# Two V transfers of group 1 made as 120 and 8 partitions each, in a chunk-attention and squared-ReLU FFN kernel on one Trainium2 core

## The chip, the core and the metric

The kernel runs on one core of a Trainium2 chip. TensorE (PE, with weight loads listed as PEld), VectorE (DVE), ScalarE (ACT) and GpSimd (POOL) run their own instruction queues; SyncE (SP) mostly issues DMA transfers, which the core's 16 DMA engines carry out. The metric is the device time of one execution in microseconds; lower is better. A time is the median of several runs. The profile and the trace come from one execution of their own.

## What is computed

The inputs are `q`, `k`, `v` of 8 batches x 8 heads x 576 positions x 64 elements in float32, and the weights `w_in` (512 x 2048) and `w_out` (2048 x 512). Attention stays within chunks of 64 positions; the FFN runs over all 4608 tokens. Cut to what matters:

```python
scores = scale * np.matmul(q_c, k_c.transpose(0, 1, 2, 4, 3))
scores = scores - np.max(scores, axis=-1, keepdims=True)
attn = np.exp(scores)
attn = attn / (np.sum(attn, axis=-1, keepdims=True) + 1e-09)
out = np.matmul(attn, v_c)
...
x = attn_out.transpose(0, 2, 1, 3).reshape(B * S, H * D)
h = np.maximum(x @ w_in, 0.0)
return (h * h @ w_out).astype(np.float32)
```

## The kernel before

**Groups and blocks.** The 4608 tokens are cut into 18 groups of 256 tokens (four chunks each), and two groups make a block of 512 tokens. For each group the kernel transposes q and k, makes the scores (`scores`, line 464), multiplies the exponentials with V (`values`, line 496), normalizes (`out_of_x`, line 438) and transposes the result x, so that the FFN can use it. The FFN of block j runs while the attention of the next blocks is made in between. From block 4 on, the FFN products are made with fewer multiplications (lines 601 to 892); the change doesn't touch that.

**Order.** The program is written with a manual schedule: the instructions of each engine run in the order in which the code emits them. The framework adds the waits between engines.

**The opening.** Lines 967 to 991 are block 0's attention, ahead of any FFN work, written out by hand. `go(pieces([0, 1]))` (line 967) issues all transfers of groups 0 and 1 on SP's queue: first q and k of both groups (line 266, four transfers of 512 KB), then V of group 0, then V of group 1, as `v_pieces` gives them. `load_w_in(0, n_cast=2)` follows, the first eighth of w_in (line 329, 512 KB, into a float32 staging tile `w_st`); GpSimd casts its first half to bf16 (line 334), ScalarE its second half (line 333). TensorE's order is then: transposes of q and k, scores of group 0 and 1, the values of group 0 in two halves, those of group 1 in two halves (`AV(1, [0])`, `AV(1, [1])`, line 510), with transposes of x in between (`transpose_x_early`, line 521), and small filler matmuls on the identity (`keep_busy`, line 433). After the last transposes come the matmuls of the first FFN (line 579), which need w_in in bf16.

**V's tiles.** The 64 rows of a chunk and four heads of 64 elements make a tile's content for one parity of the heads. The even heads of a group lie in `v_even[g % 5]`, whose two halves `[:, 0]` and `[:, 1]` hold 128 positions each; the odd heads lie in `v_odd` tiles, moved by one chunk against the even ones. A transfer of 128 partitions is 128 KB: in each partition four pieces of 256 B, one per head. For group 1 there are four transfers, in this order on SP's queue: `even[0]` (line 308, 128 partitions), `odd[0]` (line 312, 128 partitions), `even[1]` (line 308, 128 partitions), `odd[1]` (line 312, 64 partitions, 64 KB). The second half of the values, `AV(1, [1])`, reads `even[1]` and both odd tiles; the first half reads `even[0]`, `odd[0]` and a tile of group 0.

**After the opening.** Lines 993 to 1002 issue the rest of w_in, w_out and the loads of the next groups on the same queue, each w_in or w_out piece into one of five staging tiles as they come free.

Of the kernel before, what the change touches and what calls it, by code (L numbers as in the profile page):

```python
# [144 lines left out]
def kernel(  # L145
# [9 lines left out]
    nc = tc.nc  # L155

    B, H, S, D = q.shape
# [17 lines left out]
    chunks = whole[:-2] + rest + whole[-2:]  # L175
# [64 lines left out]
    v_even = [w_pool.tile([128, 2, n_hp, D + 1], FP32, name=f"ve_sb{i}") for i in range(NV)]  # L240
    v_odd = [w_pool.tile([128, n_hp, D + 1], FP32, name=f"vo_sb{i}") for i in range(NO)]
# [5 lines left out]
    def runs(g):  # L247

        for t in range(2):
            (b, s), (b1, s1) = chunks[g][2 * t:2 * t + 2]  # L250
            if b == b1:
                yield t, 0, 2 * CH, b, s
            else:
                yield t, 0, CH, b, s
                yield t, CH, CH, b1, s1
# [28 lines left out]
    odd_tile, odd_loads = {}, {}  # L284
    n_odd = 0
    for g in range(n_grp):
        if is_whole(g):
# [3 lines left out]
            b, s = chunks[g][0]  # L291
# [12 lines left out]
    def v_pieces(g):  # L304

        even, odd = [], []
        for t, p, m, b, s in runs(g):
            even.append(lambda t=t, p=p, m=m, b=b, s=s: nc.sync.dma_start(  # L308
                out=v_even[g % NV][p:p + m, t, :, 0:D],
                in_=v[b, 0::2, s:s + m, :].rearrange("h s d -> s h d")))  # L310
        for n, p, m, b, s in odd_loads[g]:
            odd.append(lambda n=n, p=p, m=m, b=b, s=s: nc.sync.dma_start(  # L312
                out=v_odd[n % NO][p:p + m, :, 0:D],
                in_=v[b, 1::2, s:s + m, :].rearrange("h s d -> s h d")))
        if g < 2:
            yield from [even[0], *odd[:-1], even[1], odd[-1]]
        else:
            yield from even + odd

# [607 lines left out]
    def pieces(grps):  # L927
        for g in grps:
            yield from qk_pieces(g)
        for g in grps:  # L930
            yield from v_pieces(g)
# [72 lines left out]
    for j in range(QUADS):  # L1004
# [33 lines left out]
        else:  # L1038
# [4 lines left out]
            if j == 2:  # L1043
                loads, go_slots = itertools.chain(*map(v_pieces, nxt), pieces(far)), [
                    *range(16), *range(27, 36)]
                slots = {SC: (6, 10), AV: (12, 22), XT: (15, 28), CQ: (20, 22), CK: (21, 24), TD: (24, 26)}
                for f in (CQ, CK, TD):
                    for i, g in enumerate(far):
                        at(slots[f][i], f, g)
                phases.append(out_j)  # L1050
            else:
                loads, go_slots = pieces(far), range(11)
                at(11, C, far[0])
                at(13, CQ, far[1])
                at(13, TD, far[0])
                slots = {SC: (2, 4), AV: (7, 10), XT: (13, 15)}
# [40 lines left out]
    for j in range(QUADS, n_blk):  # L1097
# [7 lines left out]
        if j == QUADS:  # L1105
            g = blocks[QUADS + 1][1]
# [116 lines left out]
```

## Time and profile before

| what | value |
|---|---|
| time, median of 3 runs | 279.12 us (278.87 to 279.75) |
| the profiled execution, its own time | 278.37 us |
| its span in the trace | 276.6 us |
| PE busy | 265.3 us, 96% of the span |
| DVE, ACT, POOL busy | 199.3, 170.1, 90.7 us |
| DMA | 55.07 MB moved, mean 199 GB/s |
| DMA, mean rate in the first two fortieths of the span | 216 and 260 GB/s |
| granted TensorE clock | 1.0 in every stretch |

How to read it: times are from the start of the span. A line number names the line of the kernel that issued the instruction; `SPq` is SP's issue of a transfer, `DMA` the time in which a transfer is under way. A group's line has what it writes, an arrow, what it reads, and the number of instructions; the bracket behind it gives how long the engine stood idle before it, and what ended that. A wait is put down to the one event that came last.

### The profile page before, as it was taken

The page shows a single profiled execution, that of the slowest core. Times are in us where ns is not written, and L with a number is a line of the kernel's source. Part 1 is how long each engine was busy: PE and PEld are TensorE (multiplying, and loading weights), DVE is VectorE, ACT ScalarE, POOL GpSimd, SP SyncE. Part 2 cuts the span into 40 slices and gives each one's busy share as a digit, 9 for nine tenths or more (in the row PEclk, how much of TensorE's full clock was granted, in tenths as well). Part 3 has the DMA queues.
Part 4 walks back from the last instruction along what each step waited for, and adds up shares of the span by engine and source line. Part 5 has one row for each costly group of instructions (what it writes and reads, how often), then busy time and mean ns, then how long its engine had stood idle before and what let it go on. Part 6 is the DMA issues. An engine that isn't in the chain of part 4 may idle for free.

```text
span 276.6 us, 7949 instructions
## 1 busy us (share of the span) xinstructions
PE 265.3 (96%) x3274; PEld 203.9 (74%) x3277; DVE 199.3 (72%) x365; ACT 170.1 (61%) x302; POOL 90.7 (33%) x122
## 2 busy tenths in 40 slices
PE   2889999999999999999999999999999999999994
PEld 2764445888774588447888888888898888888884
DVE  1457415999538692599989998799679877994852
ACT  1657514894458883867678765566856664756430
POOL 2048734350270012140245224551434312431600
PEclk9999999999999999999999999999999999999999
DMA  7999999999999999998999999697995330220223
GB/s 216 260 373 383 366 318 262 325 209 162 278 209 206 245 246 231 285 240 121 229 228 199 217 236 198 116 214 198 254 195 162 78 76 2 89 62 9 71 83 114
DMA packets 133943, 55.07 MB, mean 199 GB/s; under 512 B 102160, under 2 KB 129808, under 8 KB 133904
## 3 DMA queue, kind: packets, MB, share of 16 engines
q1 hardware_dynamic: 131136, 46.02, 70.9%
q0 software_dynamic: 2624, 8.39, 9.7%
q8 instruction: 26, 0.43, 0.6%
q10 hardware_dynamic: 144, 0.13, 0.1%
q14 instruction: 13, 0.11, 0.1%
HBM read 36.70 MB, written 9.44 MB: 167 GB/s over the span
## 4 chain that ended last, share of the span: by engine, by line
PE 82%; DVE 8%; DMA 4%; SPq 4%; issue 1%; ACT 0%; POOL 0%
PE ps_ffn L657 23%; PE ps_out L780 22%; PE ps_ffn L579 13%; PE ps_ffn L780 12%; PE ps_ffn L901 5%; DVE gT L598 4%; PE ps_att L510 2%; DMA w_st<-in_moe_w_in_dram 2%; PE ps_att L483 2%; PE ps_att L540 2%; DMA qkT<-qkb 2%; SPq L266 1%; SPq L308 1%; SPq L312 1%; DVE x L443 1%
## 5 line engine op out<-in xcount | busy, mean ns | idle before, releaser
L579 PE MATMUL ps_ffn<-xT,w_in_bf 128*128 128x512 bf16 (+1 forms) x328 | 58.0, 333 | 0.1
L780 PEld LDWEIGHTS <-w_st 128*128 128x128 bf16 x512 | 48.8, 98 | 6.6 <-DVE w_st L614 0.5
L665 DVE CUSTOM_DVE_ANT_0 relu<-ps_ffn,w_st 128x512 f32<-128x512 f32 x60 | 39.3, 685 | 12.8 <-PE ps_ffn L657 11.4
L598 DVE TENSOR_TENSOR gT<-relu 128x256 bf16<-128x256 bf16 (+2 forms) x68 | 34.6, 543 | 18.0 <-ACT relu L590 17.5
L579 PEld LDWEIGHTS <-w_in_bf 128*128 128x128 bf16 x328 | 31.1, 98 | 21.4 <-POOL w_in_bf L334 0.2
L590 ACT ACTIVATE relu<-ps_ffn 128x256 bf16<-128x256 f32 (+2 forms) x82 | 39.5, 502 | 10.3 <-PE ps_ffn L579 9.6
L657 PE MATMUL ps_ffn<-qk_st,w_in_bf 128*128 128x256 bf16 x240 | 35.3, 273 | 0.0
L657 PEld LDWEIGHTS <-w_in_bf 128*128 128x128 bf16 x320 | 30.6, 98 | 4.0 <-issue 0.3
L809 POOL DMA_DIRECT2D out_dram<-o_sb x24 | 17.6, 733 | 44.7 <-DVE o_sb L614 24.6
L780 PEld LDWEIGHTS <-gT 128*128 128x128 bf16 x296 | 28.6, 98 | 3.3
L780 PE MATMUL ps_out<-w_out_bf,w_st 128*128 128x256 bf16 x240 | 30.8, 273 | 0.0
L699 ACT ACTIVATE w_st<-ps_ffn 128x512 f32<-128x512 f32 x20 | 11.9, 598 | 27.5 <-PE ps_ffn L657 27.5
L443 DVE TENSOR_TENSOR x<-ps_att,recs 128x512 bf16<-128x512 f32 x36 | 24.9, 692 | 1.2
L657 PEld LDWEIGHTS <-qk_st 128*128 128x128 bf16 x240 | 22.6, 98 | 2.9
L676 POOL TENSOR_TENSOR qk_st<-relu 128x512 bf16<-128x512 f32 x10 | 10.3, 1034 | 41.6 <-DVE relu L665 38.1
L657 PE MATMUL ps_ffn<-xT,qk_st 128*128 128x256 bf16 x160 | 23.9, 273 | 0.0
L494 ACT ACTIVATE e<-ps_att 128x1024 bf16<-128x1024 f32 x18 | 18.4, 1023 | 8.6 <-PE ps_att L483 8.6
L676 POOL TENSOR_TENSOR gT<-relu 128x512 bf16<-128x512 f32 x10 | 10.3, 1033 | 36.9 <-DVE relu L665 36.9
L449 POOL CAST qkb<-qk_st 128x1024 bf16<-128x1024 f32 x12 | 14.8, 1236 | 13.3 <-DMA qk_st<-in_q_dram 13.3
L674 ACT ACTIVATE gT<-relu 128x512 bf16<-128x512 f32 x28 | 17.7, 631 | 0.0
L780 PE MATMUL ps_ffn<-w_out_bf,w_st 128*128 128x256 bf16 x144 | 17.7, 273 | 0.0
L614 DVE TENSOR_TENSOR w_st<-gT,w_st 128x1024 bf16<-128x1024 bf16 x26 | 17.5, 708 | 0.0
(92 smaller groups left out, 430.5 us busy)
## 6 DMA issues: line engine op xcount, KB each, us to landing
qk_st<-in_q_dram SPq DMA_DIRECT2D x16, 512.0 KB, 5.8
out_dram<-o_sb POOLq DMA_DIRECT2D x28, 256.0 KB, 3.9
qk_st<-in_k_dram SPq DMA_DIRECT2D x24, 256.0 KB, 5.3
ve_sb<-in_v_dram SPq DMA_DIRECT2D x32, 128.0 KB, 3.9
w_st<-in_moe_w_in_dram SPq DMA_DIRECT2D x8, 512.0 KB, 6.0
w_st<-in_moe_w_out_dram SPq DMA_DIRECT2D x8, 512.0 KB, 5.4
vo_sb<-in_v_dram SPq DMA_DIRECT2D x24, 128.0 KB, 3.3
qk_st<-in_k_dram SPq DMA_DIRECT2D x4, 512.0 KB, 5.9
```

The costliest lines, as they stand in the source:

```text
L443: nc.vector.tensor_tensor(out=x, in0=o[:, :, :, 0:D], in1=rec.to_broadcast([128, 2, n, D]), op=ALU.mult)
L494: nc.scalar.activation(out=e_out, in_=s_in, func=AF.Exp, scale=scale)
L579: nc.tensor.matmul(out=h[:, 0:n], lhsT=w_in_bf[:, dt, ft * 128:(ft + 1) * 128], rhs=xT[:, c // 128:(c + n) // 128, dt, :], start=(dt == 0) ...
L590: nc.scalar.activation(out=rl[:, 0:n], in_=h[:, 0:n], func=AF.Relu)
L598: nc.vector.tensor_tensor(out=dst, in0=src, in1=src, op=ALU.mult)
L614: nc.vector.tensor_tensor(out=out, in0=in0, in1=in1, op=op)
L657: nc.tensor.matmul(out=bank[:, f * GT:(f + 1) * GT], lhsT=a[:, dt, ft * 128:(ft + 1) * 128], rhs=b[:, :, dt, :], start=(first and f == 0 a ...
L665: nc.vector._custom_dve(TENSOR_ADD_SAT, out=out, in0=in0, in1=in1, s0=BIG, s1=0.0)
L674: engine.activation(out=dst, in_=r, func=AF.Square)
L676: engine.tensor_tensor(out=dst, in0=r, in1=r, op=ALU.mult)
L780: nc.tensor.matmul(out=out_ps, lhsT=lhsT, rhs=b[:, i, :], start=(first and i == 0 and (last or t == 0)), stop=(i == HF - 1), skip_group_ch ...
L809: dma.dma_start(out=out[t0:t0 + GT, col:col + HD].rearrange("(t p) d -> p t d", p=128), in_=o_sb.rearrange("p (t d) -> p t d", d=HD))
```

## The change

For group 0 the order stays. For group 1 the first even and the first odd transfer, 128 partitions each, are replaced by two transfers each: 8 partitions (120 to 127) and then 120 partitions (0 to 119). The two that follow, `even[1]` and `odd[-1]`, stay as they were and behind them. The other groups stay as they were.

```diff
-        if g < 2:
+        if g == 0:
             yield from [even[0], *odd[:-1], even[1], odd[-1]]
+        elif g == 1:
+            for tile_, heads, s in ((v_even[1][:, 0], 0, chunks[1][0][1]),
+                                    (v_odd[odd_loads[1][0][0]], 1, odd_loads[1][0][4])):
+                for p, m in ((120, 8), (0, 120)):
+                    yield lambda t=tile_, h=heads, s=s, p=p, m=m: nc.sync.dma_start(
+                        out=t[p:p + m, :, 0:D],
+                        in_=v[chunks[1][0][0], h::2, s + p:s + p + m, :].rearrange("h s d -> s h d"))
+            yield from (even[1], odd[-1])
         else:
             yield from even + odd
```

## The prediction

> **What bounds the kernel now.** I began with the page: the span, the shares by engine, and the DMA queues.
>
> ```profile
> span 276.6 us, 7949 instructions
> PE 265.3 (96%) x3274; PEld 203.9 (74%) x3277; DVE 199.3 (72%) x365; ACT 170.1 (61%) x302; POOL 90.7 (33%) x122
> ...
> q8 instruction: 26, 0.43, 0.6%
> ```
>
> Then busy time by stretches, cut where the first FFN matmul starts (17.42 us) and just before the end; the second column is the length, the third PE.
>
> ```profile
> 0.00:17.42 17.42, 10.63 (x244) 8.38 (x245) 6.20 (x13) 7.51 (x11) 2.13 (x24) 1.00 1.03 264
> 17.42:270.00 252.58, 251.58 (x3004) 193.04 (x3008) 191.73 (x350) 162.19 (x291) 88.53 (x98) 1.00 0.81 197
> ```
>
> From 17.42 us to 270 us TensorE is idle for 252.58 - 251.58 = 1.0 us in all. So what the opening gains or loses passes to the end almost unchanged, and whatever the change does later to SP's queue must first eat the slack of loads that already arrive in time. The question is when the first FFN matmul starts. The chain of waits, in order of time, gives one answer:
>
> ```profile
> 8.76 0.63 SPq L308
> 9.39 0.04 issue
> 9.44 0.55 SPq L312
> 9.98 0.04 issue
> 10.03 0.58 SPq L308
> 10.61 0.04 issue
> 10.65 0.60 SPq L312
> 11.26 0.04 issue
> 11.30 5.40 DMA w_st<-in_moe_w_in_dram
> 16.70 0.06 issue
> 16.75 0.62 POOL w_in_bf L334
> 17.38 0.05 issue
> 17.42 14.01 PE ps_ffn L579 x72
> ```
>
> SP issues group 1's four V transfers (8.76 to 11.26), then the first piece of w_in; it lands at 16.70, POOL casts it, PE starts. The chain shows one predecessor only. The timeline of the opening shows a second, equally late:
>
> ```profile
> 14.46 0.22 PE L510 MATMUL ps_att<-ve_sb,e 64*64 64x65 bf16 x2
> ...
> 15.11 0.69 DVE L443 TENSOR_TENSOR x<-ps_att,recs 128x512 bf16<-128x512 f32 x1
> ...
> 15.23 0.22 PE L510 MATMUL ps_att<-ve_sb,e 64*64 64x65 bf16 x2 [0.45 <-DMA ve_sb<-in_v_dram]
> ...
> 15.62 0.21 PE L510 MATMUL ps_att<-vo_sb,e 64*64 64x65 bf16 x1 [0.17 <-DMA vo_sb<-in_v_dram]
> ...
> 15.97 0.21 DVE L442 RECIPROCAL recs<-ps_att 128x8 f32<-128x8 f32 x1 [0.18 <-PE ps_att L510]
> ...
> 16.22 0.69 DVE L443 TENSOR_TENSOR x<-ps_att,recs 128x512 bf16<-128x512 f32 x1
> ...
> 16.96 0.40 PE L521 MATMUL ps_ffn<-ident,x 128*128 128x128 bf16 x4
> ...
> 17.42 2.51 PEld L579 LDWEIGHTS <-w_in_bf 128*128 128x128 bf16 x21 [0.23 <-POOL w_in_bf L334]
> ```
>
> The second half of group 1's values waits for V until 15.62, DVE normalizes until 16.22 + 0.69 = 16.91, and the last transposes end at 16.96 + 0.40 = 17.36, 0.06 us before the FFN. Two chains tie, so a gain needs both.
>
> Why is the data so late? The views merge packets, so I took this from the trace's packet records (us from the span's start):
>
> ```
> queue 8 (instruction): one packet, 16384 B, starts 12.50, takes 1.288
> 256 B packets of V: 4096 in all; 4048 of them are over by 13.41
> the other 48 start from 13.77 on and are over at 14.85, one after another
> w_in piece 0, end of each engine's part: 14.70 to 15.21 for fifteen engines, 16.30 for one
> first packet of the first q transfer: 1.87; w_in piece 0's first packet: 12.96
> ```
>
> One DMA engine stands still while it fetches instructions, with exactly 32 + 16 = 48 V packets before it: its shares of SP's last two V transfers (128 partitions x 4 heads / 16 = 32 packets, and the half-size one). It ends V 14.85 - 13.41 = 1.44 us after the others, and the first w_in piece 16.30 - 15.21 = 1.09 us after them. The queue 8 row says the same in the mean: 0.6% of 16 engines x 276.6 us, over 26 packets, is 1.0 us each, on one engine.
>
> The Trainium skill ("Runtime: NRT & Kernel Launch", section "Instruction fetch mechanics") says that each engine's program is refilled in blocks of 16 KiB, 256 instructions. The trace agrees: (3274 + 3277) / 256 = 25.6, and there are 26 packets, so these would be TensorE's, and their time is set by TensorE's progress.
>
> **The change, part by part.** It leaves the bytes alone. Four issues stand where two stood, and the two transfers that it splits are the ones *ahead* of the 48 late packets. The late ones (line 308's second, line 312's half-size one) stay as they are, on all 16 engines.
>
> *SP's issues.* No transfer of 8 or 120 partitions is in the trace. The nearest are the crowded V issues above (0.55 to 0.63, plus 0.04) and an uncrowded one:
>
> ```profile
> 33.30 0.46 SPq L308 DMA_DIRECT2D ve_sb<-in_v_dram  x1
> ```
>
> Low end: four at 0.50 from 8.76, then two at 0.50: the last two V issues start at 10.76 and 11.26, w_in at 11.76, 0.46 later than now. High end: 0.67 each, so 11.44, 12.11 and 12.78, 1.48 later. I take 0.55 each (10.96, 11.51, 12.06): the two 8-partition transfers give the queue a sixteenth of the packets, so the crowd should ease. The first transfer's first packet came 1.87 - 0.75 = 1.12 us after its issue began. So w_in's packets could start at 12.06 + 1.12 = 13.18, or 13.90 at the high end; the late engine takes them up only at 14.85. *Cost: nothing*, covered by that engine's lateness. Without this cover the other engines' end would move from 15.21 by 13.18 - 12.96 = 0.2 up to 0.9 us, still not past 16.30.
>
> *Packets.* If the freed engine is the one that fetches, it loses 64 packets, and runs out of work before 12.50. What it gains depends on how many of its last 48 pass before the fetch. The second-last V transfer, issued at 10.96, can show packets from 12.08; 0.42 us at (0.60 us per V transfer / 32 =) 19 ns each is 22 packets. With the issue ends: 32 packets (11.88) or none (12.56). The remaining ones took (14.85 - 13.77) / 48 = 22 ns each, so V would end 0.5 us earlier (0 to 0.7), and w_in behind it.
>
> *What that is worth.* DVE still works on the first half until 15.11 + 0.69 = 15.80. The second reciprocal can move from 15.97 to 15.80 at best: 0.17 us, then the products, the transposes (end 17.19) and the FFN. w_in needs only 0.17 of the 0.5 us. So -0.17 if packets pass before the fetch, 0 if none do. Both are about as likely by the row above: -0.08.
>
> *Waits.* Values of group 1 now wait for two transfers more. On PE's queue nothing shows such an extra wait alone; the nearest row is that of the waits ahead of w_in's issues (min, median, max ns):
>
> ```profile
> L329 SPq EVENT_SEMAPHORE  x4: 17/28/944, 15.8 to 19.7; - x4
> ```
>
> The 944 holds a wait for data, so I take 28 ns, two or three times: +0.06 (bounds 0 and 0.25, the mean of ten idle stretches ahead of such weight loads for no named reason).
>
> ```profile
> PEld L510 <- issue: 2.5, 10, 0.4
> ```
>
> The transfers will have landed well before 14.46 (the old ones were over by about 12.5), and behind the waiting matmuls stands all of PE's queue, so this price is paid in full.
>
> *Sum:* -0.08 + 0.06 = 0.0 us, between -0.17 and +0.25. The profiled execution took 278.37 us (span 276.6, so 1.8 us lie around it); the median shown is 279.12, 0.75 above it. I add the sum to the median: **279.1 us**.
>
> **The rivals.**
>
> *The wrong engine is freed.* Nothing in the profile numbers the engines. If the fetching engine is one of those that take the 8 partitions (4 packets each, 8 in all), it gets 8 packets more ahead of the 48: 8 x 19 to 22 ns, V and w_in about 0.2 us later, both chains: 279.3.
>
> *Slower: a narrow transfer is dear to issue.* If a transfer that doesn't fill 16 engines takes SP long, w_in is issued late and nothing covers it. It decides once w_in's first packet comes after 14.85, so its issue after 13.73, so from a mean issue of (13.73 - 8.76 - 1.2) / 4 = 0.94 us. The longest issue in this queue is a bound:
>
> ```profile
> 4.69 1.45 SPq L308
> ```
>
> Four of 1.49, then two of 0.6: w_in issued at 15.9, packets from 17.0, against 14.85 now: +2.2 us, 281.3. Against it: 1.45 stands where 512 KB transfers crowd the queue, and the same line later takes 0.46. Midway it is 280.2.
> The Trainium skill ("DMA: Bandwidth & Descriptors", section "Rules for kernel authors") speaks against splitting by partitions as such: both parts share the engines and serialize, and one 128-partition transfer is to be used. The trace's V transfers do follow each other 0.60 us apart.
>
> *It isn't 15 engines.* If the 120 partitions went over 8 engines, these would have 15 x 4 = 60 packets per transfer, 2 x 28 x 19 ns = 1.06 us more. V would end there at 14.47, still before 14.85: 279.1. Were the late engine among them, +1.06: 280.2.
> By the Trainium skill (the same page, section "Why a DMA increments its semaphore by 16 and not by 1") the number is the largest up to 16 that divides the partitions, counted from the lowest engine: 15 for 120, 8 for 8. No run here shows it. By it the sum stands if the last engine fetches, and 279.3 if one of the first eight does.
>
> *Much faster.* The three unprofiled runs are above the profiled one; if the late engine is later there by those 0.75 us and the change frees it, -0.17 - 0.75: 278.2. For it speaks only that gap; against it, that DVE's chain caps this profile at 0.17.
>
> **How the numbers follow.** A measurement of this kernel tells about 0.3% (0.84 us) from no change. Forecast, no difference that shows: 0.57. Wrong engine: 0.15 (also within). Dear issues: 0.14, of which 0.11 over 0.84. Other spread of the partitions: 0.06, of which half is slower. Much faster: 0.08. So slower 0.11 + 0.03, and 0.02 for slips on later loads: 0.16; faster 0.09, the last 0.01 for the medians' scatter; same 0.75. The likeliest case's own range is 278.7 to 279.5, 0.17 and 0.25 about the sum plus some 0.2 for a median of three. The range runs from 278.4, leaving out the far part of the fast case, to 280.4, a little past midway of the dear issues.
>
> **What would show it.** In the chain of waits and SP's timeline: w_in's first issue near 12.1, each of the four new issues near 0.55 (over 0.94 makes the slow rival). In the timeline: the second half of group 1's values starting before 15.62, the second reciprocal at 15.80, the last transposes at 16.79, the FFN at 17.25 in the good case. In the packet records: the fetch still at 12.5, and fewer than 48 V packets after it. V later than 15.62 by about 0.2 means that the wrong engine was freed. I am wrong if the FFN starts within 0.2 us of 17.42 and the time still moves by over 0.84 us: then something behind 17.42 us sets it, which the 1.0 us of idle PE time hides from me.

## The result, and the profile after

The changed kernel is slower: 279.37 us against 278.53 us at the median of 17 runs each, 0.84 us apart, and a ratio of 1.0037 with a 95% interval of 1.002 to 1.0053. Some executions of any of these kernels are 1 to 3% slower as a whole, so all ratios here compare the other, fast executions and need not be those of the medians; of the profiles used below only that of the two small transfers ahead of V is a slow one. The changed kernel's profiled execution took 280.59 us, 1.2 us above its own median, so not all that this trace shows is the change's.

From the page of the changed kernel:

```profile
span 278.8 us, 7951 instructions
...
q1 hardware_dynamic: 131150, 46.02, 71.7%
```

SP's queue moved 131136 packets before and 131150 now. Two transfers on 16 engines post 32 completions, so 32 + 14 = 46 = 2 x (15 + 8): the 120 partitions went over 15 engines and the 8 over 8. The Trainium skill's rule that the prediction quotes ("DMA: Bandwidth & Descriptors", section "Why a DMA increments its semaphore by 16 and not by 1") gives the same numbers.

The timeline of SP's issues, changed kernel (line 321 is the new one, line 337 the load of w_in):

```profile
8.76 0.87 SPq L321 DMA_DIRECT2D ve_sb<-in_v_dram  x2
9.67 0.82 SPq L321 DMA_DIRECT2D vo_sb<-in_v_dram  x2
10.64 0.40 SPq L308 DMA_DIRECT2D ve_sb<-in_v_dram  x1
11.08 0.60 SPq L312 DMA_DIRECT2D vo_sb<-in_v_dram  x1
11.73 10.07 SPq L337 DMA_DIRECT2D w_st<-in_moe_w_in_dram  x8
```

Four issues take (10.64 - 8.76) / 4 = 0.47 us each; w_in's first starts at 11.73, 0.43 us later than before. The timeline of the opening on PE, DVE and POOL:

```profile
15.80 0.69 DVE L451 TENSOR_TENSOR x<-ps_att,recs 128x512 bf16<-128x512 f32 x1
...
15.91 0.20 PEld L518 LDWEIGHTS <-e 64*64 64x64 bf16 x13 [0.26 <-DMA vo_sb<-in_v_dram]
...
16.41 0.20 DVE L450 RECIPROCAL recs<-ps_att 128x8 f32<-128x8 f32 x1
...
17.04 0.61 POOL L342 CAST w_in_bf<-w_st 128x512 bf16<-128x512 f32 x1 [14.83 <-DMA w_st<-in_moe_w_in_dram]
...
17.70 0.73 PE L587 MATMUL ps_ffn<-xT,w_in_bf 128*128 128x256 bf16 x5
```

V is waited for until 15.91 (before: 15.62), the second reciprocal starts at 16.41 (15.97), w_in's first cast at 17.04 (16.75). The first half is late too: DVE's product of it starts at 15.80 (15.11). The two chains are 0.29 to 0.44 us late, and the first FFN matmul starts at 17.70 instead of 17.42. The prediction's sign for a wrong engine, V later than 15.62, is there.

The rest of this trace's loss lies behind that. Busy time by stretches of the changed kernel, then of before (second column the length, third PE):

```profile
40.00:125.00 85.00, 82.96 (x1108) 56.88 (x1105) 58.66 (x117) 57.08 (x103) 20.75 (x24) 1.00 1.03 226
```

```profile
40.00:125.00 85.00, 84.05 (x1110) 57.46 (x1107) 60.40 (x118) 58.07 (x105) 23.25 (x25) 1.00 1.04 240
```

From 40 to 125 us PE idles for 85.00 - 82.96 = 2.04 us, against 0.95 before. The waits of that time, changed kernel, say for what:

```profile
PEld L491 <- DMA qkT<-qkb: 2.8, 3, 1.3
PE ps_att L491 <- DMA qkT<-qkb: 1.8, 3, 1.1
```

The scores of the later blocks (line 491) wait for the transposed q and k, which are loaded and transposed on the same queue. The DMA share is 1.03 there, so the load stream can hardly make up a late start; that reading was argued, not tried.

### The profile page after: what moved, and what is told of

Same layout as the page of the kernel before. It is cut to its first block, busy times and chain, and to the rows that moved or that the text cites. A ratio compares the mean times of both kernels' runs of the same rounds, so it can differ in the third digit from the quotient of the medians.

```text
span 278.8 us, 7951 instructions
## 1 busy us (share of the span) xinstructions
PE 266.7 (96%) x3274; PEld 204.6 (73%) x3277; DVE 199.3 (71%) x365; ACT 170.3 (61%) x302; POOL 89.2 (32%) x122
## 3 DMA queue, kind: packets, MB, share of 16 engines
q1 hardware_dynamic: 131150, 46.02, 71.7%
## 4 chain that ended last, share of the span: by engine, by line
PE 77%; DMA 10%; DVE 5%; SPq 5%; issue 1%; ACT 1%; ACTq 0%
PE ps_ffn L665 22%; PE ps_out L788 21%; PE ps_ffn L587 15%; PE ps_ffn L788 8%; PE ps_ffn L909 5%; DMA qkT<-qkb 5%; DMA vo_sb<-in_v_dram 3%; DVE gT L606 2%; PE ps_att L518 2%; PE ps_att L491 2%; DMA qk_st<-in_q_dram 2%; SPq L266 2%; SPq L279 1%; PE ps_att L548 1%; SPq L468 1%; DVE x L451 1%
## 5 line engine op out<-in xcount | busy, mean ns | idle before, releaser
L606 DVE TENSOR_TENSOR gT<-relu 128x256 bf16<-128x256 bf16 (+2 forms) x68 | 32.2, 502 | 19.8 <-ACT relu L598 19.3
L457 POOL CAST qkb<-qk_st 128x1024 bf16<-128x1024 f32 x12 | 13.0, 1080 | 22.1 <-DMA qk_st<-in_q_dram 21.9
```

What stands on the lines that cost most here:

```text
L606: nc.vector.tensor_tensor(out=dst, in0=src, in1=src, op=ALU.mult)
```

## The experiments

Theory A: the two more issues ahead of w_in delay the load stream. Rivals: B, chance; C, the uneven shares; D, other semaphores for the later transfers; E, the address of the tiles; F and G, whether the fetching engine was among the freed ones. All ratios are to the kernel before on the same chip, with their 95% interval.

**The changed kernel again (first of two).** No edit.

> The changed kernel once more, for a second profile of its opening and of the scores after it. Theory A (late loads): SP's load stream leaves the opening some 0.4 us late and, with the DMA engines over 90% busy up to 130 us, stays late, so that PE waits for the transposes of q and k at the scores near 70 us and 115 us: ratio 1.002 to 1.006, the first FFN near 17.7 us, over 2 us of weight loads of the scores waiting for those transposes in all (0.8 in the profile of before, 3.2 in that of after). Theory B (chance): the 3.2 us were one bad draw; the second profile shows about 1 us, and the ratio is within 0.998 to 1.003.

Measured: 1.0007 (0.9969 to 1.0046); the time alone doesn't tell A from B. First FFN at 17.63. But the scores hardly waited; instead PE lost its time near 20 us. The waits from 17 to 30 us of this run:

```profile
POOL w_in_bf L342 <- DMA w_st<-in_moe_w_in_dram: 17.9, 6, 14.8
PEld L587 <- POOL w_in_bf L342: 1.6, 2, 1.4
PE ps_ffn L587 <- POOL w_in_bf L342: 1.1, 1, 1.1
```

The FFN waited for the second piece of w_in. The expected place was wrong, the kind of wait (a late load) not.

**64 and 64 partitions.**

```diff
-                for p, m in ((120, 8), (0, 120)):
+                for p, m in ((64, 64), (0, 64)):
```

> The same two transfers split into 64 and 64 partitions: as many issues as in the changed kernel, but every transfer on all 16 engines, with the packets shared evenly. Theory A (two more issues delay the load stream): as the changed kernel, ratio 1.002 to 1.006, w_in's first issue near 11.7 us or later. Theory C (the uneven shares, 15 and 8 engines, do it): as before, ratio 0.998 to 1.002, though w_in is issued as late.

Measured: 1.0052 (1.0017 to 1.0087), with w_in's first issue at 13.68 and the first FFN at 18.62. C falls: even shares are no better. The ratio need not be the issues' alone: in its profile the granted clock was 0.58 from 18 to 22 us, against 1.0 before.

**Two small transfers, first attempt, at two places.** They go into new tiles of 32 B a partition (`e3_lanes` among the w_out loads, `e4_tiny` ahead of group 1's V):

```diff
+    spare = [const_pool.tile([16, 8], FP32, name=f"spare{i}") for i in range(2)]
...
+        if i < 2:
+            nc.sync.dma_start(out=spare[i], in_=v[0, 0, 0:16, 0:8])
```

> Before, with two transfers of 512 B added among the w_out loads near 22 to 25 us, where SP waits for staging tiles anyway (4.8 us in five waits): no issue of the opening moves, but each later transfer gets another of the semaphores that transfers take in turn, as in the changed kernel. Theory D (waits that fall on other semaphores make the later stream late): ratio 1.002 to 1.006. Theory A: no change, 0.998 to 1.002, w_in's first issue at 11.3 us, the first FFN at 17.4 us.

> Before, with two transfers of 512 B added just ahead of group 1's V: the two more issues of the changed kernel at the same place, without its split of V. Theory A: as the changed kernel, ratio 1.002 to 1.006, w_in's first issue near 11.7 us. Theory C: as before, 0.998 to 1.002.

Measured: 1.0158 (1.0098 to 1.0218) and 1.0264 (1.0211 to 1.0316), more than any theory had. But already the first q and k transfers, issued as before, were slower: by the packet records they ended 1.8 us apart in place of 1.5. The two runs tested something else as well, the address of all later tiles. Both were made again into a tile that exists, and the address alone:

**The address alone.** The two tiles allocated and cleared by GpSimd, no further transfer.

> Before, with two tiles of 32 B a partition allocated ahead of the weights' and staging tiles and cleared by GpSimd, but no further transfer: all later tiles lie 64 B further. Theory E (the address makes packets slow): 512 B packets of q and k at 31 ns in place of 27, q and k landing 1.8 us apart in place of 1.5, ratio 1.01 to 1.03. Otherwise 0.998 to 1.002.

Measured: 1.0151 (1.0104 to 1.0198). The transposes of q and k in PE's timeline, run with the shifted tiles:

```profile
5.03 1.06 PE L403 MATMUL ps_ffn<-ident,qk_st 128*64 128x128 bf16 x16 [5.03 <-DMA qk_st<-in_q_dram]
6.82 1.07 PE L403 MATMUL ps_ffn<-ident,qk_st 128*64 128x128 bf16 x16 [0.73 <-DMA qk_st<-in_k_dram]
8.63 1.06 PE L403 MATMUL ps_ffn<-ident,qk_st 128*64 128x128 bf16 x16 [0.74 <-DMA qk_st<-in_q_dram]
```

and before:

```profile
4.68 1.06 PE L400 MATMUL ps_ffn<-ident,qk_st 128*64 128x128 bf16 x16 [4.68 <-DMA qk_st<-in_q_dram]
6.20 1.06 PE L400 MATMUL ps_ffn<-ident,qk_st 128*64 128x128 bf16 x16 [0.45 <-DMA qk_st<-in_k_dram]
7.69 1.07 PE L400 MATMUL ps_ffn<-ident,qk_st 128*64 128x128 bf16 x16 [0.43 <-DMA qk_st<-in_q_dram]
```

One transfer after the other lands 1.8 us apart in place of 1.5; a 512 B packet takes 31 ns in place of 27. Theory E holds, and the first attempts alone say nothing on A or D. Beside the address alone (1.0151), the transfers among the w_out loads add nothing (1.0158); those ahead of V add 1.1%, but in that profile the granted clock was also down to 0.95 from 40 to 80 us.

**The small transfers into an existing tile.** `e6_tiny` ahead of group 1's V, `e9_lanes` among the w_out loads:

```diff
+            for x in kept_sb if g else ():
+                yield lambda x=x: nc.sync.dma_start(out=x[0:16, 0:8], in_=v[0, 0, 0:16, 0:8])
```

```diff
+        if i < 2:
+            nc.sync.dma_start(out=kept_sb[i][0:16, 0:8], in_=v[0, 0, 0:16, 0:8])
```

> The two transfers of 512 B ahead of group 1's V again, now into a tile that exists already, so that no tile lies at another address than in before. The q and k transfers should land as in before (4.3, 5.8, 7.3, 8.8 us by the packet records). Theory A, two more issues: ratio 1.002 to 1.005, w_in's first issue near 11.7 us. Theory E, that the address alone made the first attempt slow: ratio under 1.006 where that had 1.026; without theory A 0.998 to 1.002.

> The two transfers of 512 B among the w_out loads again, now into a tile that exists already. q and k land as in before (4.3 to 4.4, 5.8, 7.3 to 7.5 us by the packet records). Theory D (the later transfers get other semaphores, and that makes them late): 1.002 to 1.006. Theory A (issues ahead of w_in's first): 0.998 to 1.002.

Measured: 1.0047 (1.0016 to 1.0078) ahead of V, 0.9974 (0.9951 to 0.9996) among the w_out loads. Two issues without any change to V cost what the change costs, if they stand ahead of w_in; behind it they cost nothing (0.9974 is even just under the range expected). D falls. One thing was missed: ahead of V, w_in's first issue came at 13.30, not near 11.7; the table below shows which issue stopped there.

**Before again.** No edit.

> The kernel before, unchanged, for a second profile and for what the comparison makes of no change. All theories: ratio 0.997 to 1.003. Theory A (the changed kernel's load stream is late, and the scores near 70 and 115 us wait for it) wants this profile to look like the first of before: first FFN within 0.1 us of 17.4, fewer than 1.2 us of the scores' weight loads waiting for transposes. Theory B (chance: w_in's packets and the transposes land late in some executions of either kernel) wants it to differ by as much as the two profiles of the changed kernel did, about 1 us in what PE has lost by 30 us.

Measured: 1.0014 (0.9979 to 1.0049), which is what five rounds make of no change. First FFN at 17.33; 0.9 us of waits for transposes. PE starts group 2 within 0.1 us of the first profile (39.06 against 39.13), though w_in's third piece landed at 20.11 us against 19.35.

**The 8-partition transfers on ACT (twice).**

```diff
-                    yield lambda t=tile_, h=heads, s=s, p=p, m=m: nc.sync.dma_start(
+                    yield lambda t=tile_, h=heads, s=s, p=p, m=m: (nc.scalar if p else nc.sync).dma_start(
```

> The changed kernel with the two 8-partition transfers issued by ACT at its start: SP has as many issues as before, the shares of the DMA engines are those of the changed kernel. Theory A: back to before, ratio 0.998 to 1.002, w_in's first issue at 11.3 us. Theory F (the wrong engine is freed, and the packets that it doesn't carry cost time on the others): still slower, 1.002 to 1.004, with V's last packets at 14.9 us or later.

> The two 8-partition transfers on ACT once more, next to the changed kernel on the same chip. Theory A: 0.997 to 1.001, below the changed kernel by 0.002 or more. Theory B (chance): the two within 0.001.

Measured: 0.9984 (0.9958 to 1.001) and 0.999 (0.9966 to 1.0014). The second stood beside the changed kernel on the same chip, which had 1.004 (1.001 to 1.007): medians 278.62 against 280.13 us, twelve runs each. Taking the two issues off SP takes the loss away. In one thing the first run missed: w_in's first issue was at 13.00 there, not 11.3. That led to the table below.

**Six small transfers.** As `e6_tiny`, with six.

> Before, with six transfers of 512 B in place of two ahead of group 1's V. Theory A by the dose: w_in's first issue 1.5 to 3 us later than 11.3, the first FFN after 18 us, ratio 1.006 to 1.015. Theory B: as the two transfers, within 1.006.

Measured: 1.0155 (1.0111 to 1.02), w_in's first issue at 15.02, the first FFN at 20.16: A by its direction, but beyond what it expected (up to 1.015, and an issue up to 3 us later). A part of it may be the clock's, which was granted at 0.50 from 18 to 22 us in its profile; that part was not separated.

**88 and 40 partitions, on SP, and with the 40 on ACT.**

```diff
-                for p, m in ((120, 8), (0, 120)):
+                for p, m in ((88, 40), (0, 88)):
```

> The split at 88 and 40 partitions. If 88 go over 11 engines and 40 over 10, as 120 went over 15 and 8 over 8 by the packet count, five engines carry nothing of the two transfers, and those with both carry 48 packets of each in place of 32. Theory G (the engine that fetches instructions near 12 us is one of the five freed): at most 48 V packets remain on it when the others are done, V ends under 14.8 us and the second reciprocal starts at 15.8 us. Theory F (it is one of the others): over 48 packets remain, V ends at 15 us or later. The time: 1.002 to 1.006 by theory A in both.

> 88 partitions on SP, 40 on ACT: SP has as many issues as before, and the five highest engines, the fetching one among them by the run with 88 and 40, carry nothing of the 88. Theories A and G: V is not waited for, the second reciprocal at 15.8 to 16.0 us, ratio 0.997 to 1.001. If freeing an engine costs time by itself: over 1.002.

Measured: 1.0026 (0.9995 to 1.0058) and 1.0033 (1.0006 to 1.006). In the first, 131146 packets are 2 x (11 + 10) completions. V's last packet ended at 14.50, only 9 packets were left after 14.4, and nothing waits for V. From its timeline:

```profile
11.38 1.72 SPq L312 DMA_DIRECT2D vo_sb<-in_v_dram  x1
...
15.38 0.69 DVE L451 TENSOR_TENSOR x<-ps_att,recs 128x512 bf16<-128x512 f32 x1
15.99 0.20 DVE L450 RECIPROCAL recs<-ps_att 128x8 f32<-128x8 f32 x1
...
18.34 0.66 PEld L587 LDWEIGHTS <-w_in_bf 128*128 128x128 bf16 x7 [1.14 <-POOL w_in_bf L342]
```

The early end of V alone doesn't show theory G, that the fetching engine is among the five freed: the first run with 8 partitions on ACT, with the changed kernel's shares, ended V at 14.43, and in both the issue of the last V transfer ended only at about 13 us. The run with 40 on ACT, which had issued all of V before SP stopped, supports G: at 13.9 us 28 V packets were left, against 56 in the second profile of before, whose fetch began 0.1 us later. In the changed kernel the engine was not freed: at 13.9 us, with the other engines done, 60 V packets were still to come (65 in its second profile, 44 before), more than the 48 that a freed engine could have. By the Trainium skill's rule that the prediction quotes (the freed engines are the highest) the fetching engine would then be one of 11 to 14; that it is the same one in each execution is assumed. But freeing it gained nothing. In the run with 88 and 40 on SP the FFN waited 1.14 us for w_in, whose first issue came at 13.13, and the second reciprocal came at 15.99, not at the 15.8 expected, as the first half was late as well (DVE's product at 15.38, before 15.11). The run with 40 on ACT missed its expectation (second reciprocal 16.16, ratio over 1.002, where the rival that freeing an engine costs time by itself had put it; no run excludes that rival). It has as many issues on SP as before and is slower all the same; w_in's first issue waited there too (11.72 to 13.72), and each of up to ten engines carries 48 packets of a transfer in place of 32.

**Scores of block 2 two slots later, in the changed kernel and in before.**

```diff
-                for slot, f in ((16 + 4 * i, C), (21 + 4 * i, TD), (36 + i, SC), (38 + 2 * i, AV),
-                                (41 + 2 * i, XT)):
+                for slot, f in ((16 + 4 * i, C), (21 + 4 * i, TD), (38 + i, SC), (40 + 2 * i, AV),
+                                (43 + 2 * i, XT)):
```

> The changed kernel with block 2's scores, values and transposes two slots later, so that PE has about 1 us more of FFN matmuls to do before it needs the transposed q and k near 70 us. Theory A (part of the loss is that wait): ratio to before 0.999 to 1.002, below the changed kernel's 1.0037, and under 0.3 us of waits for the transposes near 70 us. If the loss lies in the opening alone: unchanged, 1.002 to 1.005.

> Before, with the same two slots. If before itself sometimes waits there: 0.996 to 0.999; if its transposes are in time in most executions: 0.999 to 1.001.

Measured: 1.0116 (1.0086 to 1.0146) and 1.0045 (1.0024 to 1.0066), both missed. The waits from 70 to 90 us, before with the later scores:

```profile
PE ps_ffn L579 <- ACT xT L545: 1.1, 1, 1.1
```

The next block's FFN now waits for its x. The edit brought a wait of its own and tells nothing on the old one. The two are still a pair that differs by the change alone: 1.0116 against 1.0045.

**The changed kernel a third time.**

> The changed kernel a third time, next to the three that follow. Theory A: ratio 1.001 to 1.005, w_in's first issue 0.4 us or more after 11.3, the first FFN at 17.5 to 17.8 us or, if the fetch begins before that issue, at 18 or later. Whether PE waits near 70 us for transposes, near 20 us for w_in, or not at all tells if the rest of the loss has one place.

Measured: 1.004 (1.001 to 1.007). First FFN at 17.18, earlier than expected (18 or later if the fetch begins ahead of w_in's first issue, as it did, at 11.27 against 11.74), and then PE stands still for w_in. Its timeline:

```profile
17.18 1.92 PE L587 MATMUL ps_ffn<-xT,w_in_bf 128*128 128x256 bf16 x16
19.25 2.02 POOL L342 CAST w_in_bf<-w_st 128x512 bf16<-128x512 f32 x3 [2.13 <-DMA w_st<-in_moe_w_in_dram]
...
20.05 1.25 PE L587 MATMUL ps_ffn<-xT,w_in_bf 128*128 128x512 bf16 x5 [0.96 <-POOL w_in_bf L342]
```

**One table from the traces.** "Stopped issue" is the issue on SP that lasts over 1.2 us near the fetch; w_in 0, 1, 2 are the pieces of w_in. "GB/s" is what the DMA engines moved from 12 to 16 us, the last number of lines like these, of before and of the changed kernel's third profile:

```profile
12.00:16.00 4.00, 2.86 (x75) 2.09 (x74) 2.51 (x6) 2.19 (x3) 0.00 (x0) 1.00 1.18 293
```

```profile
12.00:16.00 4.00, 3.31 (x78) 2.36 (x76) 2.57 (x7) 2.19 (x3) 0.00 (x0) 1.00 0.98 218
```

The last column is where PE starts the transposes of group 2 (lines 400 and 408 in the kernels before and changed), a fixed point of the program behind the first FFN products. The three runs with shifted tiles are left out. All times in us, from the records and timelines:

| kernel | fetch | stopped issue, its end | w_in 0 issued | first FFN | GB/s | group 2 |
|---|---|---|---|---|---|---|
| before | 12.50 to 13.78 | w_in 2, 14.20 | 11.30 | 17.42 | 293 | 39.13 |
| before, later scores | 12.40 to 13.69 | w_in 2, 14.10 | 11.32 | 17.30 | 287 | 39.01 |
| 8 partitions on ACT, second | 12.45 to 13.77 | w_in 2, 14.18 | 11.27 | 17.34 | 299 | 39.05 |
| before again | 11.69 to 12.97 | w_in 1, 13.46 | 11.28 | 17.33 | 259 | 39.06 |
| changed | 11.99 to 13.32 | w_in 1, 13.74 | 11.73 | 17.70 | 266 | 39.41 |
| changed, second | 12.02 to 13.33 | w_in 1, 13.75 | 11.85 | 17.63 | 261 | 40.63 |
| changed, third | 11.27 to 12.60 | w_in 0, 13.00 | 11.74 | 17.18 | 218 | 40.01 |
| changed, later scores | 11.87 to 13.12 | w_in 0, 13.52 | 12.06 | 17.51 | 201 | 39.47 |
| small transfers behind | 11.60 to 12.70 | w_in 0, 13.09 | 11.57 | 17.25 | 237 | 40.62 |
| 88, with 40 on ACT | 11.59 to 13.32 | w_in 0, 13.72 | 11.72 | 17.46 | 183 | 41.34 |
| 8 partitions on ACT, first | 11.19 to 12.59 | last V, 12.96 | 13.00 | 17.98 | 176 | 39.74 |
| 88 and 40 | 11.40 to 12.66 | last V, 13.09 | 13.13 | 18.34 | 175 | 40.31 |
| 64 and 64 | 11.92 to 13.20 | last V, 13.63 | 13.68 | 18.62 | 122 | 42.00 |
| small transfers ahead | 11.22 to 12.21 | third V, 12.61 | 13.30 | 18.06 | 157 | 39.91 |
| six small transfers | 11.37 to 12.39 | a small one, 12.74 | 15.02 | 20.16 | 95 | 43.54 |

While the engine fetches, SP's queue comes to a stop, and it goes on 0.35 to 0.49 us after the fetch ends, in all eighteen traces. What was issued ahead of the stop keeps the DMA engines at work meanwhile; the earlier in the queue the stop falls, the less they move: 287 to 299 GB/s with w_in 2 stopped, 259 to 266 with w_in 1, 183 to 237 with w_in 0, 122 to 176 with a V transfer, 95 with a small one. Group 2 tends to start later in the same order, though the ranges overlap: 39.01 to 39.13, 39.06 to 40.63, 39.47 to 41.34, 39.74 to 42.00, 43.54. The loss can't be read piece by piece: in the changed kernel's third profile w_in 0 was held until 13.00 and still landed earlier than before (16.46 against 16.70), while w_in 3, issued as early as before (14.20 against 14.24), landed at 22.15 against 20.68.

The changed kernel issues w_in 0 at least 0.4 us later than the first four rows, so a fetch at the same time catches an earlier piece. But the fetch itself began anywhere from 11.19 to 12.50, which decides as much: in the changed kernel's four profiles at 11.79 in the mean, in the four with before's opening (before, later scores, again, small transfers behind) at 12.05. Whether the change moves the fetch too, or this is chance, so few profiles don't tell.

## Why the prediction was wrong, step by step

**What bounds the kernel: right for the start, too short behind it.** The two chains that tie at 17.4 us set the first FFN in the other profiles too, though there one can end well ahead of the other (with 88 and 40, PE waits 1.14 us for w_in alone). But the prediction read the 1.0 us of idle PE time as a sign that nothing after 17.42 us could add a loss. In the changed kernel's profiles PE stopped at one or two of three places: at the first FFN, for w_in's second piece, or for the transposes near 70 us. The third of them is close to what the prediction named as its own sign of being wrong: the first FFN is 0.24 us earlier than before, and by group 2 PE is 0.88 us later.

**SP's issues: the size right, the price wrong. This is the step that failed.** w_in's first issue was forecast at 12.06 (11.76 to 12.78) and came at 11.73 (11.74 to 12.06 in the other profiles), so a narrow transfer is cheap to issue. "Cost: nothing, covered by that engine's lateness" is what does not hold. The cover was worked out for the first piece of w_in alone, and SP was taken to go on issuing while the engine fetches. It stops instead, and with every issue ahead of w_in less of the load stream is on its way when it does. Four runs show that the two issues have a price: two alone 1.0047, six 1.0155 (with the lower clock), two taken off SP 0.9984 and 0.999. That the price comes by way of the stop is argued from the table; no run took the stop away. PE reaches group 2 at (39.41 + 40.63 + 40.01 + 39.47) / 4 = 39.88 in the profiles with the change, against 39.07 in the three with before's opening and nothing else changed ahead of that point. That is 0.8 us, and the medians differ by 0.84 us. A fourth profile with before's opening, that of the small transfers behind, is at 40.62 and lowers this to 0.4 us: so few profiles don't give the size by themselves.

**Packets: the rival was right that the wrong engine is freed.** The prediction gave it 0.15. That the fetching engine was not freed is shown by the 60 and 65 packets left. The rival's price, 8 packets more on it, doesn't follow, as the 8-partition parts went over 8 engines, by the Trainium skill's rule the lowest; its 279.3 was near the measured 279.37 for another reason.

**What it is worth: the limit right, the 0.17 us not seen.** In the run with 88 and 40, with V in time, the second reciprocal starts about when DVE is done with the first half, as predicted. But the first half was late too, so it started at 15.99, no earlier than the 15.97 before.

**Waits of the values: not told apart.** The 0.06 us is below what these runs resolve.

**The other rivals.** Dear issues: no, 0.47 us each. Other than 15 engines: no, by the packet count. Much faster: no. The range held the time; the forecast itself, no difference that shows, did not.

**What stays open.** Why some pieces of w_in land up to 2 us late in the changed kernel, where their issue was at most 1.3 us late or not late at all, and why the place where PE stops differs from one execution to the next, were not settled. A single profile doesn't stand for its kernel's median either: the small transfers behind and the first run with 8 partitions on ACT have a late group 2 in the table and no loss in their ratios (0.9974, 0.9984). And the run with 40 on ACT loses (1.0033) with no more issues on SP than before. Nor did a version come out clearly ahead of before: the one with the 8-partition transfers on ACT is within its interval of no change.

## What to carry to other kernels

A transfer's issue isn't free because the data behind it are late: ask what else waits in the same queue, and for how long that queue can stand still. Where DMA engines are busy over 90% of the time, cost a shift of the load stream at each later wait for a load, not at the next one alone. When an experiment adds a tile, put it where no other tile moves, or run the new address by itself.

## What the runs showed of the hardware

- The first fetch of 16384 B, which in the opening keeps one DMA engine for 1.0 to 1.7 us, goes with a stop of SP's issues until 0.35 to 0.49 us after its end, in all eighteen traces. The fetch alone doesn't make the stop: in five traces an issue lay wholly inside a later fetch, near 19 to 22 us, and took its usual 0.37 us. That in the crowded opening the fetching engine's queue is full by then would explain it; this was argued, not tried. The Trainium skill ("Runtime: NRT & Kernel Launch", section "Instruction fetch mechanics") calls the cost of crossing such a block mostly hidden. In this opening it isn't: in the first profile of before it holds one engine's V back by 1.44 us, and the values wait for V until 15.62.
- That fetch began anywhere from 11.2 to 12.5 us in the fifteen profiles of the table, whose kernels have the same instructions on TensorE up to then.
- Tiles that lie two small tiles (32 B a partition each) further made 512 B packets of the loads take 31 ns in place of 27, and the kernel 1.5% slower (1.0104 to 1.0198).
- A transfer of 120, 88, 40 and 8 partitions posted completions on 15, 11, 10 and 8 engines, by the count of packets.
